# Projections and query features on half rows of the array, in a kernel of feature-map attention and a gated MLP

## The chip, the cores and the metric

The kernel runs on one core of a Trainium2 chip. The metric is the device time of one execution in microseconds. Before the change it is 278.79 us, the median of three runs (278.53 to 278.94).

## What is computed

The inputs are q, k and v for 8 batches, 8 heads, 576 tokens and 64 channels, and a projection of 64 by 128. Keys and queries are projected, the largest magnitude of a token's projection is taken off, and both signs go through the exponential, which gives 256 features.

```python
def phi(x):
    proj = np.einsum('bhsd,df->bhsf', x, w_phi)
    proj = proj - np.max(np.abs(proj), axis=-1, keepdims=True)
    return np.concatenate([np.exp(proj), np.exp(-proj)], axis=-1)
q_p, k_p = (phi(q), phi(k))
kv = np.einsum('bhsf,bhsd->bhfd', k_p, v)
z = np.sum(k_p, axis=2)
num = np.einsum('bhsf,bhfd->bhsd', q_p, kv)
den = np.einsum('bhsf,bhf->bhs', q_p, z)[..., None] + 1e-06
x = num / den                     # heads side by side: 576 x 512 a batch
h = np.maximum(x @ w_in, 0.0)     # 1024 wide: u and v
v_n = (v - mu) / np.sqrt(var + 1e-06)
v_s = np.einsum('ts,bsd->btd', w_spatial, v_n) + b_spatial[None, :, None]
out = (u * v_s) @ w_out
```

## The kernel before

The attention is cut into 36 units, listed in `units`. A *pair unit* holds two heads of one batch and 512 of its 576 tokens: for each head four blocks of 128 tokens, eight blocks in all. A *tail unit* holds the last 64 tokens of two batches for all eight heads, again eight blocks of 128 rows. There are 32 pair units and 4 tail units. The hand-written `ORDER` says what `step(i)` issues, and for which unit: each stage has a lag (`LAGS`), so that one step projects unit i, transposes the maxima of unit i - 1, makes the query features of unit i - 2 and the attention of unit i - 3. The MLP of a batch (`b_tasks`: `b_v` at L447, `b_u` at L515, `b_s` at L536, `b_o` at L561) is put into `queue` when its attention is done, and `fill(share)` issues some of it between the attention stages. The share beside each name in `ORDER` sets how much.

The stages that matter here:

- `a_transpose` (L259, L261) and `cross` bring 64 channels of two token blocks onto the 128 partitions: block 2j ("even") on partitions 0 to 63, block 2j + 1 ("odd") on 64 to 127. The result is `kT` or `qT`, four columns of blocks. For batches 0 and 1 and the tails, TensorE transposes and VectorE or ScalarE copies; from batch 2 (`XB`) a DMA on SP's queue transposes.
- `by_token` (L266) projects: one column of blocks is the stationary operand, and `wphi2`, 128 rows by 256 columns, is streamed through. Its upper left and lower right quarters hold the projection and the others zeros, so one matmul of 256 columns gives both blocks. A PSUM bank takes four blocks in token order.
- `a_keys` reads each of two key banks by a VectorE maximum (`mk`, L278) and two ScalarE exponentials (`kf`, L281). `a_scale` makes the factors of the maxima (`em`, L301) and POOL multiplies the values by them (`vs`, L306 and L308). `a_queries` takes the query maxima from two banks (`mq`, L292) and writes each as a bf16 value and its remainder into 16 columns of `mhl` (L295 and L296: VectorE in the first five units, POOL after them).
- `a_max_t` transposes `mhl` on TensorE (L327). Early and tail units copy 16 rows to `mT` (L333). The others are `merged`: the maxima are copied four times side by side into partitions of `qT` that are not needed (L330), and into those of a second arrangement of the queries, `qE` (a `qt` tile, L331), which `q_even` fills by a DMA on SP's queue one step ahead.
- `a_qfeat` projects the queries again, transposed, and takes off the maxima. A merged unit uses `wm`, which holds the projection and the rows of -1 for the maxima in one stationary operand: eight matmuls of 128 columns (L344). An early pair unit uses two matmuls of 256 columns and four of 128 per half (L348, L352), a tail unit sixteen of 128 (L357, L359). Each half fills one bank, read by two ScalarE exponentials (`qf`, L365).
- `a_kv` (L378, L380) sums keys and values, `a_num` (L398) and `tail_num` (L426) make the numerators, `norm` (L388, L389) divides, and `tail_x_t` (L439, L441) transposes the tails' result. It follows `a_qfeat` directly in the step that ends a batch.

All PSUM tiles share one tag of eight banks, which are handed out in turn. Two engines' accesses to one bank are put in an order by semaphores, two readers' as well. `pin` keeps an instruction in its place in the program, and its instructions have line L61.

The output of a batch is made by `b_o`: four matmuls of 512 columns, a copy by VectorE and ScalarE in turn (L564), and a DMA of 256 KB on SP's queue (L570). `b_o_tail` does it for the tails with two DMAs (L576). For the last batch `out_tasks` gives the four blocks and then the tails.

Of the kernel before, what the change touches and what calls it, by code (L numbers as in the profile page):

```python
# [8 lines left out]
FP32 = mybir.dt.float32  # L9
# [7 lines left out]
def kernel(  # L17
# [15 lines left out]
    nc = tc.nc  # L33
# [134 lines left out]
    wm = cpool.tile([P, H, F], BF16)  # L168
    sel1 = cpool.tile([P, H], BF16)
    sel = cpool.tile([P, H, F], BF16)  # L170
    pin(nc.vector.tensor_tensor)(out=sel1, in0=ident[:, 0:H], in1=ident[:, H:2 * H], op=ALU.add)
# [18 lines left out]

    def alternate(t, i):
        return t.rearrange("p (j two) f -> p j two f", two=2)[:, :, i, :]

    for i in range(2):
        pin(nc.scalar.copy)(out=alternate(wm, i),
                            in_=wphi2[:, i * F:(i + 1) * F].unsqueeze(1).to_broadcast([P, NP, F]))

    def maxima_rows(i):
        r = slice((1 - i) * D, (1 - i) * D + 2 * H)
        pin(nc.scalar.copy)(out=alternate(wm[r], i), in_=alternate(sel[0:2 * H], i))  # L200
# [40 lines left out]
    def merged(u):  # L241
        return u["pair"] and u["b"] >= XB

    def q_even(u):
        u["qE"] = qts[u["i"] % len(qts)]
        pin(nc.sync.dma_start)(out=u["qE"][0:D], in_=u["qT"][0:D])
# [16 lines left out]
    def by_token(xT, half):  # L263
        ps = psum.tile([P, 4, F], FP32, tag="bank", name="ps")
        for x in range(2):
            nc.tensor.matmul(out=ps[:, 2 * x:2 * x + 2, :], lhsT=xT[:, 2 * half + x, :], rhs=wphi2,  # L266
                             start=True, stop=True)
        return ps

    def a_keys(u):  # L270

        u["mk"] = small.tile([P, H], FP32, tag="mk", name="mk")
        u["kf"] = feat.tile([P, 2, H, F], BF16, tag="kf" if u["pair"] else "kf_t", name="kf",
                            bufs=4 if u["pair"] else 2)
        for half in range(2):
            pk = by_token(u["kT"], half)
            hs = slice(4 * half, 4 * half + 4)
            nc.vector.tensor_reduce(out=u["mk"][:, hs], in_=pk, axis=AX.X, op=ALU.max,  # L278
                                    apply_absolute_value=True)
            for s, sc in ((0, 1.0), (1, -1.0)):  # L280
                nc.scalar.activation(out=u["kf"][:, s, hs, :], in_=pk, func=AF.Exp, bias=0.0, scale=sc)  # L281

    def a_queries(u):

        m, early = mhl[u["i"] % NM], u["i"] < EARLY
        if not early:
            mq = small.tile([P, H], FP32, tag="mq", name="mq")
        for half in range(2):
            pq = by_token(u["qT"], half)
            if early and half == 0:  # L290
                mq = pq[:, 0, 0:H]
            nc.vector.tensor_reduce(out=mq[:, 4 * half:4 * half + 4], in_=pq, axis=AX.X, op=ALU.max,  # L292
                                    apply_absolute_value=True)
        eng = nc.vector if early else nc.gpsimd
        eng.tensor_copy(out=m[:, 0:H], in_=mq)  # L295
        eng.tensor_tensor(out=m[:, H:2 * H], in0=mq, in1=m[:, 0:H], op=ALU.subtract)  # L296
# [28 lines left out]
    def a_max_t(u):  # L325
        pt = psum.tile([P, P], BF16, tag="bank", name="pt")
        nc.tensor.transpose(out=pt, in_=mhl[u["i"] % NM], identity=ident)  # L327
        if merged(u):
            odd, even = u["qT"][0:2 * H], u["qE"][D:D + 2 * H]
            nc.vector.tensor_copy(out=odd, in_=pt[0:2 * H, :].unsqueeze(1).to_broadcast([2 * H, 4, P]))  # L330
            nc.vector.tensor_copy(out=even, in_=pt[0:2 * H, :].unsqueeze(1).to_broadcast([2 * H, 4, P]))  # L331
            return
        nc.vector.tensor_copy(out=mT[u["i"] % NM][0:2 * H, :], in_=pt[0:2 * H, :])  # L333

    def a_qfeat(u):

        m = mT[u["i"] % NM]
        u["qf"] = []
        for half in range(2):
            pq = psum.tile([P, 4, P], FP32, tag="bank", name="pq")  # L340
            if merged(u):
                for par, src in enumerate((u["qE"], u["qT"])):
                    for x in range(2):
                        nc.tensor.matmul(out=pq[:, 2 * par + x, :], lhsT=wm[:, 4 * half + 2 * x + par, :],  # L344
                                         rhs=src[:, 2 * half + x, :], start=True, stop=True)
            elif u["pair"]:
                for par in range(2):
                    nc.tensor.matmul(out=pq[:, 2 * par:2 * par + 2, :], lhsT=wphi2[:, par * F:(par + 1) * F],  # L348
                                     rhs=u["qT"][:, 2 * half:2 * half + 2, :], start=True, stop=False)
                    for x in range(2):  # L350
                        j = 4 * half + 2 * x + par
                        nc.tensor.matmul(out=pq[:, 2 * par + x, :], lhsT=sel[:, j, :], rhs=m,  # L352
                                         start=False, stop=(x == 1))
            else:
                for x in range(4):
                    h = 4 * half + x
                    nc.tensor.matmul(out=pq[:, x, :], lhsT=wphi2[:, (h % 2) * F:(h % 2 + 1) * F],  # L357
                                     rhs=u["qT"][:, h // 2, :], start=True, stop=False)
                    nc.tensor.matmul(out=pq[:, x, :], lhsT=sel[:, h, :], rhs=m, start=False, stop=True)  # L359
            if u["pair"]:  # L360
                qf = feat.tile([P, 2, 4, P], BF16, tag="qf", name="qf", bufs=7)
            else:
                qf = feat.tile([P, 2, 4, P], BF16, tag="qf_t", name="qf_t", bufs=4)
            for s, sc in ((0, 1.0), (1, -1.0)):
                nc.scalar.activation(out=qf[:, s], in_=pq, func=AF.Exp, bias=0.0, scale=sc)  # L365
            u["qf"].append(qf)
# [204 lines left out]

    def b_o_tail(g, bls):
        r = slice(bls[0] * TL, (bls[-1] + 1) * TL)
        ob = o_mm(lambda dc: gs[g]["uTt"][:, dc, r], r)
        for bl in bls:
            nc.sync.dma_start(out=out[2 * g + bl, T0:S, :], in_=ob[bl * TL:(bl + 1) * TL, :])  # L576
# [21 lines left out]
    def out_tasks(b):  # L598
        ts = [(MM, lambda j=j: b_o(b, j)) for j in range(NB)]
        if b % 2:  # L600
            ts.append((MM, lambda: b_o_tail(b // 2, [0, 1])))
        return ts

    def b_tasks(b):
# [11 lines left out]
        for y in range(NB):  # L616
# [5 lines left out]
    ORDER = (("keys", 0.375), ("queries", 0.25), ("attention", 0), ("sums", 0.25),  # L622
             ("next", 0.125), ("features", 0), ("out", 0), ("maxima", 0))
# [24 lines left out]
    def step(i):  # L648
# [5 lines left out]
        for what, share in ORDER:  # L654
            for u in units[max(0, i - 5):i + 2]:
# [3 lines left out]
                if what == "keys":  # L659
                    a_keys(u)  # L660
# [3 lines left out]
                elif what == "queries":  # L664
                    a_queries(u)
# [27 lines left out]
    at(0, maxima_rows, 0)  # L693
    at(1, load_v, 1)
    at(1, maxima_rows, 1)
# [20 lines left out]
    for u in units:  # L716
        if merged(u):
            at(u["i"] - 1, q_even, u)
# [50 lines left out]
```

## Time and profile before

| | |
|---|---|
| time, median of 3 runs | 278.79 us (278.53 to 278.94) |
| the profiled execution | 277.52 us, span 275.7 us from the first to the last instruction |
| maxima of keys and queries (L278, L292) on DVE | 72 of 681 ns; 62 of 678 and 10 of 690 ns |
| exponentials of keys and queries (L281, L365) on ACT | 144 of 638 ns; 128 of 625 and 16 of 608 ns |
| projections (L266) on PE | 288 matmuls of 128x256 |
| value scaling (L306) on POOL | 64 of 1042 ns |
| granted TensorE clock | 1.0 of full speed throughout |

PE is TensorE, DVE VectorE, ACT ScalarE, POOL GpSimd and SP SyncE. In a line of the profile the output stands left of the arrow and the inputs right of it, then the shapes, the count after an x, busy time in us and mean time in ns. A matmul's shape begins with the rows and columns of the array that its stationary operand takes (64*128 is half the rows), then partitions and columns streamed. Matmuls are pipelined: one takes some 0.2 us from start to modelled end, while the next can start long before. The timeline merges equal instructions in a row, and its second column is the time from the first one's start to the last one's end.

### The profile page before, as it was taken

What the parts mean: (1) busy time and instruction counts of PE and PEld (TensorE: products, weight loads), DVE (VectorE), ACT (ScalarE), POOL (GpSimd) and SP (SyncE); (2) the same over time, 40 slices, a digit from 0 to 9 for tenths busy, and PEclk for the clock granted to TensorE, in tenths of its full rate; (3) what the DMA queues carried; (4) which work ended last, traced back from release to release, by engine and by line L of the source; (5) the groups of instructions that cost most, each with busy time, mean ns of one, the idle gap of its engine ahead of it and who ended that gap; (6) DMA issues with size and microseconds to landing.
All of it is one profiled execution on the core that took longest, in us unless ns stands there. A gap on an engine that the chain in (4) does not pass through costs nothing.

```text
span 275.7 us, 8138 instructions
## 1 busy us (share of the span) xinstructions
PE 254.7 (92%) x3007; PEld 171.3 (62%) x3047; DVE 236.5 (86%) x614; ACT 218.1 (79%) x501; POOL 184.4 (67%) x312
## 2 busy tenths in 40 slices
PE   3778999999999999999998999999998999999993
PEld 2467776777665766666665775766655765554441
DVE  7989999879999889998889899988898897565751
ACT  7898999797698978999798979998798977633511
POOL 7999899999569945897787954997347632410200
PEclk9999999999999999999999999999999999999999
DMA  7999999999999997999999998899744301211115
GB/s 209 230 228 146 164 155 113 181 208 122 202 200 219 232 212 133 232 176 199 156 110 221 258 183 146 171 233 176 104 89 118 88 2 73 81 40 40 76 40 190
DMA packets 84840, 42.43 MB, mean 154 GB/s; under 512 B 51840, under 2 KB 80192, under 8 KB 84800
## 3 DMA queue, kind: packets, MB, share of 16 engines
q1 hardware_dynamic: 60240, 30.95, 54.5%
q0 software_dynamic: 24400, 10.89, 38.5%
q8 instruction: 24, 0.39, 0.6%
q14 instruction: 16, 0.13, 0.2%
q10 hardware_dynamic: 160, 0.07, 0.1%
HBM read 32.85 MB, written 9.44 MB: 153 GB/s over the span
## 4 chain that ended last, share of the span: by engine, by line
PE 70%; ACT 14%; DVE 11%; issue 3%; ACTq 0%; DVEq 0%
PE pv L447 10%; PE ps L536 10%; PE po L561 9%; PE pu L515 8%; PE ps L266 7%; ACT kf L281 7%; PE pv L378 4%; PE pn L398 4%; ACT qf L365 4%; DVE mk L278 3%; PE pq L344 3%; PE ps L537 2%; PE pn L426 2%; ACT vr L449 1%; PE pu L527 1%
## 5 line engine op out<-in xcount | busy, mean ns | idle before, releaser
L306 POOL TENSOR_TENSOR vs<-v_f,em 128x512 bf16<-128x512 f32 x64 | 65.4, 1042 | 27.8 <-ACT em L301 25.3
L281 ACT ACTIVATE kf<-ps 128x512 bf16<-128x512 f32 x144 | 75.4, 638 | 6.5 <-DVE mk L278 6.5
L365 ACT ACTIVATE qf<-pq 128x512 bf16<-128x512 f32 x128 | 66.6, 625 | 9.6 <-PE pq L344 7.5
L278 DVE TENSOR_REDUCE mk<-ps 128x4 f32<-128x512 f32 x72 | 46.3, 681 | 0.7
L292 DVE TENSOR_REDUCE mq<-ps 128x4 f32<-128x512 f32 x62 | 39.9, 678 | 2.2 <-PE ps L266 2.0
L561 PE MATMUL po<-w_out_bf,uT 128*128 128x512 bf16 x120 | 31.9, 379 | 1.4 <-ACT kf L281 0.8
L461 POOL TENSOR_TENSOR rs<-var,neghalf 64x1 f32<-64x1 f32 (+1 forms) x16 | 12.8, 797 | 30.5 <-DVE var L456 30.3
L536 PE MATMUL ps<-w_spT,vn 128*128 128x512 bf16 x119 | 32.5, 379 | 0.5
L450 DVE BATCH_NORM_STATS2 stats<-vr 128x6 f32<-128x512 bf16 (+1 forms) x40 | 26.7, 684 | 6.5 <-ACT vr L449 6.2
L447 PE MATMUL pv<-w_in_bf,xT 128*128 128x512 bf16 x117 | 30.7, 379 | 1.2 <-ACT kf L281 0.6
L515 PE MATMUL pu<-xT,w_in_bf 128*128 128x512 bf16 x119 | 31.1, 379 | 0.5 <-issue 0.2
L449 ACT ACTIVATE vr<-pv 128x512 bf16<-128x512 f32 (+1 forms) x40 | 23.8, 620 | 8.9 <-PE pv L447 8.1
L539 DVE TENSOR_TENSOR uT<-ps,uT 128x512 bf16<-128x512 f32 x32 | 22.0, 687 | 8.5 <-PE ps L537 7.6
L378 PE MATMUL pv<-vs,kf 128*128 128x66 bf16 x512 | 24.5, 193 | 1.3 <-ACT kf L281 1.1
L389 DVE TENSOR_TENSOR x<-pn,rc 128x256 bf16<-128x256 f32 x64 | 25.0, 416 | 0.3
L398 PEld LDWEIGHTS <-qf 128*128 128x128 bf16 x512 | 20.2, 97 | 7.4 <-issue 1.7
L517 ACT ACTIVATE uT<-pu 128x512 bf16<-128x512 f32 x32 | 19.7, 643 | 6.3 <-PE pu L515 3.2
L378 PEld LDWEIGHTS <-kf 128*128 128x128 bf16 x512 | 21.7, 97 | 3.6 <-issue 2.9
L398 PE MATMUL pn<-kv,qf 128*128 128x66 bf16 x512 | 21.9, 193 | 0.9 <-ACT kf L281 0.3
L380 PE MATMUL pv<-vst,kf 128*128 128x66 bf16 x128 | 21.2, 192 | 1.4 <-POOL vst L61 1.4
L564 ACT COPY ob<-po 128x512 f32<-128x512 f32 x18 | 11.0, 613 | 14.3 <-PE po L561 8.8
L467 POOL TENSOR_SCALAR vn<-vr,rs 128x512 bf16<-128x512 bf16 x28 | 21.2, 764 | 0.9
(130 smaller groups left out, 562.6 us busy)
## 6 DMA issues: line engine op xcount, KB each, us to landing
out_dram<-ob SPq DMA_DIRECT2D x32, 256.0 KB, 2.7
v_f<-in_v_dram SPq DMA_DIRECT2D x14, 512.0 KB, 5.6
k_bf<-in_k_dram POOLq DMA_DIRECT2D x14, 256.0 KB, 6.3
q_bf<-in_q_dram POOLq DMA_DIRECT2D x14, 256.0 KB, 5.9
qt<-qT_b SPq DMA_DIRECT2D x24, 64.0 KB, 4.2
v_tl<-in_v_dram SPq DMA_DIRECT2D x8, 128.0 KB, 5.9
v_f<-in_v_dram SPq DMA_DIRECT2D x1, 1024.0 KB, 8.8
w_in_bf<-in_moe_w_in_dram POOLq DMA_DIRECT2D x2, 512.0 KB, 7.0
```

Source lines behind the costliest of these rows:

```text
L278: nc.vector.tensor_reduce(out=u["mk"][:, hs], in_=pk, axis=AX.X, op=ALU.max, apply_absolute_value=True)
L281: nc.scalar.activation(out=u["kf"][:, s, hs, :], in_=pk, func=AF.Exp, bias=0.0, scale=sc)
L292: nc.vector.tensor_reduce(out=mq[:, 4 * half:4 * half + 4], in_=pq, axis=AX.X, op=ALU.max, apply_absolute_value=True)
L306: nc.gpsimd.tensor_tensor(out=vs[:, s, :, 0:D], in0=st[u["b"]]["v"][:, pj * H:(pj + 1) * H, :], in1=em[:, s, :].unsqueeze(2).to_broadcast( ...
L365: nc.scalar.activation(out=qf[:, s], in_=pq, func=AF.Exp, bias=0.0, scale=sc)
L378: nc.tensor.matmul(out=pv[:, hh, s, :], lhsT=u["kf"][:, s, 4 * hh + c, :], rhs=u["vs"][:, s, 4 * hh + c, :], start=(c == 0), stop=False)
L398: nc.tensor.matmul(out=pn[:, pos, :], lhsT=u["qf"][hh][:, s, pos, :], rhs=d["kv"][:, 2 * u["pj"] + hh, s, :], start=(s == 0), stop=(s == 1))
L447: nc.tensor.matmul(out=pv[r], lhsT=lhs(kc), rhs=w_in_bf[:, kc, HALF:DFF], start=(kc == 0), stop=(kc == KC - 1))
L450: nc.vector.bn_stats(out=stats[r], in_=dst[r])
L515: nc.tensor.matmul(out=pu, lhsT=w_in_bf[:, kc, dc * P:(dc + 1) * P], rhs=d["xT"][:, kc, :], start=(kc == 0), stop=(kc == KC - 1))
L536: nc.tensor.matmul(out=ps, lhsT=d["vn"][:, sp, cs], rhs=w_spT[:, sp, 0:T0], start=(sp == 0), stop=False)
L561: nc.tensor.matmul(out=po[r], lhsT=lhs(dc), rhs=w_out_bf[:, dc, :], start=(dc == 0), stop=(dc == KC - 1))
```

## The change

- **Projections on half rows.** `by_token` now takes even and odd blocks by matmuls of 64 rows and 128 columns each: rows 0 to 63 for even, 64 to 127 for odd, in turn. Even blocks go to one bank, odd ones to another. Keys and queries of a unit are projected together into four banks (`a_project`), and the stage "queries" leaves `ORDER`.
- **Readers by parity.** `a_readers` issues: maxima of the even keys on DVE, exponentials of the odd keys on ACT, maxima of the even queries, exponentials of the even keys, maxima of the odd keys, maxima of the odd queries.
- **Maxima doubled.** The maxima and remainders are written twice into `mhl` (columns 0 to 15 and 64 to 79), so that one transpose puts them on both halves of the partitions. One copy of 80 rows into `mT` follows, for every unit.
- **Query features.** All units use one form: per half, two matmuls of 64 rows and 256 columns with the projection, and four of 64 rows and 128 columns with `sel`; even and odd blocks in two banks. `wm`, `merged`, `q_even`, `qE` and the 24 transfers go.
- **Order.** The share 0.25 of "queries" moves to "maxima", behind the transpose.
- **The end.** The last batch's tails are put second among its outputs, and its last block is made in two halves of 256 columns: one copied by ACT and sent from ACT's queue, the other copied by DVE and sent from SP's.

```diff
-    def by_token(xT, half):
-        ps = psum.tile([P, 4, F], FP32, tag="bank", name="ps")
-        for x in range(2):
-            nc.tensor.matmul(out=ps[:, 2 * x:2 * x + 2, :], lhsT=xT[:, 2 * half + x, :], rhs=wphi2,
-                             start=True, stop=True)
+    def by_token(xT):
+        ps = [psum.tile([P, 4, F], FP32, tag="bank", name="ps") for _ in range(2)]
+        for j in range(4):
+            for y in range(2):
+                r = slice(y * D, (y + 1) * D)
+                nc.tensor.matmul(out=ps[y][:, j, :], lhsT=xT[r, j, :], rhs=wphi2[r, y * F:(y + 1) * F],
+                                 start=True, stop=True)
         return ps
...
+    def a_project(u):
+        u["pk"], u["pq"] = by_token(u["kT"]), by_token(u["qT"])
...
+        most(parity(mk, 0), u["pk"][0])
+        features(1)
+        most(mq[:, 0:4], u["pq"][0])
+        features(0)
+        most(parity(mk, 1), u["pk"][1])
+        most(mq[:, 4:8], u["pq"][1])
         eng = nc.vector if early else nc.gpsimd
-        eng.tensor_copy(out=m[:, 0:H], in_=mq)
-        eng.tensor_tensor(out=m[:, H:2 * H], in0=mq, in1=m[:, 0:H], op=ALU.subtract)
...
+        eng.tensor_copy(out=twice[0], in_=mq)
+        eng.tensor_tensor(out=twice[1], in0=mq, in1=twice[0], op=ALU.subtract)
...
-        if merged(u):
-            odd, even = u["qT"][0:2 * H], u["qE"][D:D + 2 * H]
-            nc.vector.tensor_copy(out=odd, in_=pt[0:2 * H, :].unsqueeze(1).to_broadcast([2 * H, 4, P]))
-            nc.vector.tensor_copy(out=even, in_=pt[0:2 * H, :].unsqueeze(1).to_broadcast([2 * H, 4, P]))
-            return
-        nc.vector.tensor_copy(out=mT[u["i"] % NM][0:2 * H, :], in_=pt[0:2 * H, :])
+        n = D + 2 * H
+        nc.vector.tensor_copy(out=mT[u["i"] % NM][0:n, :], in_=pt[0:n, :])
...
+        pqs = [psum.tile([P, 2, 2, P], FP32, tag="bank", name="pq") for _ in range(2)]
+        sides = [(par, slice(par * D, (par + 1) * D)) for par in range(2)]
         for half in range(2):
...
+            for par, r in sides:
+                nc.tensor.matmul(out=pqs[par][:, half], lhsT=wphi2[r, par * F:(par + 1) * F],
+                                 rhs=u["qT"][r, 2 * half:2 * half + 2, :], start=True, stop=False)
+            for x in range(2):
+                for par, r in sides:
+                    nc.tensor.matmul(out=pqs[par][:, half, x, :], lhsT=sel[r, 4 * half + 2 * x + par, :],
+                                     rhs=m[r], start=False, stop=(x == 1))
...
-    ORDER = (("keys", 0.375), ("queries", 0.25), ("attention", 0), ("sums", 0.25),
-             ("next", 0.125), ("features", 0), ("out", 0), ("maxima", 0))
+    ORDER = (("keys", 0.375), ("attention", 0), ("sums", 0.25),
+             ("next", 0.125), ("features", 0), ("out", 0), ("maxima", 0.25))
...
+        if b == B - 1:
+            ts = ts[:1] + ts[-1:] + ts[1:NB - 1] + [(MM, lambda: b_o_last(b, NB - 1))]
```

## The prediction

> **What bounds the kernel now.** I read the page's busy table first, then a table of busy time by stage, the timeline around single steps, the groups kept apart by shape, and the waits.
>
> ```profile
> PE 254.7 (92%) x3007; PEld 171.3 (62%) x3047; DVE 236.5 (86%) x614; ACT 218.1 (79%) x501; POOL 184.4 (67%) x312
> ```
>
> The average says "all three are full". The stages say more (columns: microseconds, then busy PE, weight loads, DVE, ACT, POOL):
>
> ```profile
> 15.00:30.00 15.00, 11.95 (x195) 9.80 (x192) 14.06 (x42) 14.29 (x39) 13.24 (x20) 1.00 0.96 169
> 90.00:120.00 30.00, 29.55 (x377) 20.38 (x380) 27.88 (x74) 26.43 (x65) 22.50 (x39) 1.00 1.18 196
> 150.00:180.00 30.00, 29.68 (x359) 20.15 (x365) 27.73 (x73) 26.97 (x65) 21.94 (x37) 1.00 1.13 198
> ```
>
> Up to 30 us ACT and DVE are full and PE waits. From 30 to 230 us PE is busy 193.3 of 200 us: it is the bound, with DVE (182.6) and ACT (173.6) close behind. So I price PE by the pace of its starts (a busy span holds the pipeline's latency) and treat DVE and ACT as slack of about 9% and 13%.
>
> ```profile
> 118.31 0.28 PE L344 MATMUL pq<-qt,wm 128*128 128x128 bf16 x2
> 118.42 0.28 PE L344 MATMUL pq<-qT_b,wm 128*128 128x128 bf16 x2
> 118.53 0.28 PE L344 MATMUL pq<-qt,wm 128*128 128x128 bf16 x2
> 118.65 0.28 PE L344 MATMUL pq<-qT_b,wm 128*128 128x128 bf16 x2
> 118.76 0.22 PE L327 MATMUL pt<-ident,mhl 128*128 128x128 bf16 x1
> 118.81 0.60 PE L266 MATMUL ps<-wphi,kT_b 128*128 128x256 bf16 x4
> ```
>
> Eight matmuls of 128 columns take 118.76 - 118.31 = 0.45 us, 0.056 each. Four of 256 columns span 0.60, one alone 0.273 (group L266), so they start (0.60 - 0.273)/3 = 0.109 apart. The weight loads hide behind them.
>
> **What the Trainium skill says.** "TensorEngine Tiling (Array Packing)", Key Properties: tiles run independently, but a change of tiling mode drains the engine. The kernel before has such changes, where the tail transposes of 64 rows stand between full-array work:
>
> ```profile
> 104.74 0.28 PE L344 MATMUL pq<-qT_b,wm 128*128 128x128 bf16 x2
> 104.95 0.29 PE L439 MATMUL pt<-ident,xt 64*128 64x64 bf16 x4
> 105.17 0.23 PE L327 MATMUL pt<-ident,mhl 128*128 128x128 bf16 x1
> ```
>
> The second L344 starts at 104.74 + 0.056 = 104.80; at its pace L439 would start at 104.85, and starts at 104.95. L439's last starts at 104.95 + 0.29 - 0.19 = 105.05, its pace is 0.03, and L327 comes at 105.17. A change costs 0.10 going in and 0.09 coming out: 0.19 us a round trip. The trace agrees and gives the price.
>
> "TensorE: Matmul & The Clock Gate", Measured speedup vs the span model: a group of row tiles lasts one matmul plus about 4 ns for each further tile; 3.07 times is measured for four. No row tiles run side by side in this trace, but column tiles do:
>
> ```profile
> 52.26 0.40 PE L236 MATMUL pt<-ident,wsp 128*128 128x128 bf16 x4
> 52.72 0.41 PE L236 MATMUL pt<-ident,wsp 128*64 128x128 bf16 x8
> ```
>
> Eight matmuls on half arrays take as long as four on the whole: they run in pairs. That is my reason to expect pairs on rows.
>
> "PSUM — Partial Sum Buffer", PSUM bank collisions raise a hardware error: two engines may not be in one bank at once, readers included, so software orders ACT behind DVE. The trace agrees:
>
> ```profile
> ACT kf L281 <- DVE mk L278: 6.5, 13, 0.8
> ```
>
> **The change part by part.** It is 36 units: 8 early pair units, 24 later ones (batches 2 to 7), 4 tail units.
>
> *Projections.* Before: 8 matmuls of 256 columns, 8 x 0.109 = 0.872 us a unit. After: 16 of 128 columns on half the rows, alternating between halves and banks. Bounds: perfect pairs 8 x 0.056 = 0.45; no pairing 16 x 0.056 = 0.90. I take the skill's 4 ns: 8 x 0.060 = 0.48 (estimate), plus one round trip 0.19 = 0.67. Gain 0.20 a unit, 36 x 0.20 = 7.3 us.
>
> *Query features.* After, for every unit, per half: a pair of 256 columns (0.109 + 0.004) and two pairs of 128 (0.120); twice that plus 0.19 is 0.656 us. Before: late units 8 x 0.056 = 0.447, so they lose 0.21 x 24 = 5.0; early pair units 4 x 0.109 + 8 x 0.056 = 0.884, gaining 0.23 x 8 = 1.8; tail units 16 x 0.056 = 0.894, gaining 0.24 x 4 = 1.0. The later units used one matmul where there are now two; the halves only pay that back.
>
> *Mode changes saved.* At a batch's end the tail transposes (L439) follow the features directly and are now in the same mode: 8 x 0.19 = 1.5 us.
>
> PE sum: -7.3 + 5.0 - 1.8 - 1.0 - 1.5 = -6.6 us. By place: before the late units start (about 60 us) 10 x 0.20 + 1.8 + two tails' 0.5 + 0.4 = 4.7; after, 26 x 0.20 - 5.0 + 0.5 + 1.1 = 1.8 us.
>
> *Maxima.*
>
> ```profile
> L331 DVE COPY qt<-pt 16x512 bf16<-16x512 bf16 x24 | 10.0, 415 | 0.4
> L330 DVE COPY qT_b<-pt 16x512 bf16<-16x512 bf16 x24 | 9.6, 399 | 4.2 <-PE pt L327 4.2
> L333 DVE COPY mT<-pt 16x128 bf16<-16x128 bf16 x12 | 2.4, 198 | 0.0
> ```
>
> 24 times 0.415 + 0.399 becomes 0.198 (80 rows instead of 16, the same elements per row): 14.8 us off DVE, none of it on the path while PE is the bound; it is slack. The doubled split is two small operations in the same number (L295, L296, 0.19 and 0.20 on POOL); twice the elements is at most the 0.209 of the 128x32 cast at L308: nothing, POOL idles 28 us for L306 alone. The transpose stays one matmul.
>
> *Transfers.* 24 copies of 64 KB (4.2 us each to land) leave SP's queue with their 0.54 us issues. SP also issues the cross transposes, value loads and outputs; they move up by that. The copies landed ahead of their use, since L344 shows no wait on DMA: 0 on the path, up to 1 us gain.
>
> *Start.* ACT loses four copies for wm: two of 0.57 at 5.74, while it would wait anyway, and two of 0.60 at 9.39 and 12.36, where ACT and DVE are the bound: -1.2. DVE gains two small additions for the selectors (0.24 each) before the first key cast, on DVE's unbroken chain: +0.5 unless the load's landing hides it. ACT's first key exponentials no longer follow DVE into the bank: -0.5. Sum -1.2.
>
> *Readers and order.* Exponentials and maxima keep number and size; strided 128-element blocks cost nothing (the alternating wm copies took 0.61, contiguous exponentials 0.63). New waits: DVE reads k0, q0, then k1, which ACT holds for two exponentials (L281, 0.638 span, 0.52 apart: 1.1 us); ACT reads k1, then k0, behind DVE's 0.68. Behind DVE's wait stand the second maxima, the split on POOL, then normalisation and statistics; PE waits for these through banks. With level engines both waits are near zero. Four banks are filled at once, and the last is read 2.7 us later; before, the query banks were drained in 1.4. Bounds: it removes ACT's 6.5 us of waits, or adds up to 1 us a unit. I take a net gain of 1 us out of the 6.7 us PE idles between 30 and 230.
>
> *The end.*
>
> ```profile
> 271.27 0.58 ACT L564 COPY ob<-po 128x512 f32<-128x512 f32 x1 [1.14 <-PE po L561]
> 271.88 1.11 SPq L576 DMA_DIRECT2D out_dram<-ob  x2
> ```
>
> The last copy becomes half as wide (0.42 by L389's 128x256) and one issue follows it, not two: -0.16 - 0.55 = -0.7.
>
> Sum on the path: start -1.2; 30 to 60 us a third of the 4.7, since DVE (27.4 of 30) and ACT (26.1) are near: -1.6; late units -1.8; waits -1.0; end -0.7: -6.3 us. Against the span of 275.7 that gives 269.4. The runs have a median of 278.79 (this execution counts 277.52 with its start and end outside the span), so 278.79 - 6.3 = 272.5.
>
> **The rivals.** (1) *No pairing.* Then projections cost 1.09 (+0.21 x 36 = 7.7), late features 0.884 + 0.19 - 0.447 = +0.63 x 24 = 15, the other units 12 x 0.18 = 2.2, less 1.5: +23 us, about 300. Against it: the banks are split by half, and the column pairs above. 8%. (2) *A new wait replaces DVE's work* (slower). DVE stands at k1's maxima while ACT is still in query exponentials or evacuations. Its slack is about 0.4 us a unit and the copies free 0.6: from an ACT lag of 1.1 us the wait reaches PE, and every further 0.1 us costs 26 x 0.1 = 2.6. At 1.4 us: +7.8 - 5.3 (the gain without the 1.0 of waits) = +2.5, 281. For it: at 118.80 to 121.19 ACT runs four query exponentials and an evacuation before the keys projected at 118.81. Against: work now stands between features and keys (the share moved to "maxima"). 12%. (3) *Little.* The bank wait eats 3 to 5 us: -2, 277. 15%. (4) *More.* PE's idle time goes and pairs are perfect (0.056): -11, 268. 10%. (5) Nothing: 3%, within 0.2%, about what a measurement here tells from no change.
>
> **The numbers.** The forecast has 52%. Faster 0.52 + 0.15 + 0.10 = 0.77; same 0.03; slower 0.12 + 0.08 = 0.20. The range of 267 to 281 leaves out the unpaired case and the far ends of (2) and (4). The forecast's own range is 269 to 275.5.
>
> **What would show it.** Right: projection and feature groups marked 64*128, starts in pairs a few ns apart, a gap near 0.1 on either side; sixteen matmuls in about 0.5 us; DVE's busy time near 222, ACT's near 216; PE still the fullest engine from 60 to 230; the chain's end shorter by 0.7. Wrong: starts 0.056 apart within a pair; DVE's k1 maxima waiting for ACT by over 1 us a unit; PE waiting for banks that ACT or DVE holds.

## The result, and the profile after

The changed kernel takes 275.74 us (median of three runs, 275.18 to 276.07), against 278.87 for the kernel before, with one run more than in the table ahead: a ratio of 0.9884, 95% interval 0.9857 to 0.9911, so 3.2 us less by the ratio. A fourth run took 280.17 us in a slower state that several kernels show at times, and such runs are left out here and below. The profiled executions have spans of 275.7 and 273.4 us, 2.3 apart; what follows is accounted against these 2.3. The forecast of 272.5 stood for 6.3.

The engines' busy times, first line of the page after:

```profile
PE 251.7 (92%) x3419; PEld 154.3 (56%) x3419; DVE 223.3 (82%) x593; ACT 215.9 (79%) x497; POOL 183.6 (67%) x312
```

DVE has lost 13.2 us, ACT 2.2, PE 3.0. The same three stages as before (microseconds, then busy PE, weight loads, DVE, ACT, POOL):

```profile
15.00:30.00 15.00, 11.72 (x189) 8.89 (x188) 12.49 (x35) 12.49 (x33) 12.63 (x18) 1.00 0.92 162
90.00:120.00 30.00, 29.00 (x410) 17.13 (x410) 25.34 (x69) 25.80 (x63) 24.34 (x41) 1.00 1.37 193
150.00:180.00 30.00, 29.98 (x428) 18.14 (x427) 25.81 (x70) 26.80 (x64) 24.42 (x40) 1.00 1.07 179
```

Later on PE is full as before, with more slack on DVE. In the first stage, though, ACT is at 12.49 of 15 where it had 14.29, and DVE at 12.49 where it had 14.06: what was full at the start is full no longer. The timeline of PE around one late unit's features and another's projections:

```profile
118.38 0.28 PE L336 MATMUL pq<-qT_b,wphi 64*128 64x256 bf16 x2
118.50 0.28 PE L340 MATMUL pq<-mT,sel 64*128 64x128 bf16 x4
...
118.93 0.23 PE L325 MATMUL pt<-ident,mhl 128*128 128x128 bf16 x1
...
119.96 0.40 PE L254 MATMUL ps<-wphi,kT_b 64*128 64x128 bf16 x8
120.19 0.39 PE L254 MATMUL ps<-wphi,qT_b 64*128 64x128 bf16 x8
120.51 0.39 PE L546 MATMUL po<-w_out_bf,uT 128*128 128x512 bf16 x1
```

Sixteen projections take 120.51 - 119.96 = 0.55 us, the change of mode behind them included; without it that is 0.46, where sixteen unpaired ones at 0.056 each would take 0.90. The single records show the two of a pair 2 to 4 ns apart and the next pair 56 ns on. Features take 118.93 - 118.38 = 0.55, again with the change of mode.

How far each unit is behind the kernel before, by the start of its key projections in the two traces:

| unit | 0 | 1 | 3 | 6 | 11 | 20 | 30 | 35 |
|---|---|---|---|---|---|---|---|---|
| start before, us | 5.76 | 8.66 | 15.19 | 30.12 | 60.75 | 118.81 | 186.22 | 219.81 |
| after minus before, us | +0.46 | +1.27 | +1.82 | +3.34 | +1.89 | +1.15 | -0.66 | -2.43 |

The change loses 3.3 us at the start, wins 1.5 between 30 and 61 us and 4.3 between there and 220. The gain is real and larger than it looks; more than half of it is paid back in advance.

### The profile page after: what moved, and what is told of

It reads as the page before. It is cut to its first block, busy times and chain, and to the rows that moved or that the text cites. A ratio compares the mean times of both kernels' runs of the same rounds, so it can differ in the third digit from the quotient of the medians.

```text
span 273.4 us, 8788 instructions
## 1 busy us (share of the span) xinstructions
PE 251.7 (92%) x3419; PEld 154.3 (56%) x3419; DVE 223.3 (82%) x593; ACT 215.9 (79%) x497; POOL 183.6 (67%) x312
## 4 chain that ended last, share of the span: by engine, by line
PE 65%; ACT 17%; DVE 8%; POOL 4%; DMA 2%; issue 2%; SPq 0%; POOLq 0%; ACTq 0%
PE ps L521 10%; PE po L546 10%; PE pv L432 9%; PE pu L500 7%; ACT qf L350 7%; ACT kf L279 6%; PE ps L254 4%; PE pv L363 4%; PE pn L383 4%; PE pq L336 3%; PE ps L522 3%; PE pq L340 2%; DVE stats L435 2%; DMA first<-in_k_dram 2%; DVE mk L275 2%
## 5 line engine op out<-in xcount | busy, mean ns | idle before, releaser
L279 ACT ACTIVATE kf<-ps 128x512 bf16<-128x512 f32 x144 | 76.3, 653 | 3.7 <-PE ps L254 3.6
L275 DVE TENSOR_REDUCE mk<-ps 128x4 f32<-128x512 f32 x72 | 49.1, 681 | 11.7 <-PE ps L254 7.0
L275 DVE TENSOR_REDUCE mq<-ps 128x4 f32<-128x512 f32 x62 | 41.1, 678 | 0.0
L521 PE MATMUL ps<-w_spT,vn 128*128 128x512 bf16 x128 | 33.1, 380 | 0.9 <-POOL vn L452 0.6
L500 PE MATMUL pu<-xT,w_in_bf 128*128 128x512 bf16 x128 | 32.2, 379 | 0.3 <-DVE mk L275 0.3
L432 PE MATMUL pv<-w_in_bf,xT 128*128 128x512 bf16 x128 | 31.8, 379 | 0.0
L434 ACT ACTIVATE vr<-pv 128x512 bf16<-128x512 f32 (+1 forms) x40 | 25.0, 629 | 7.6 <-PE pv L432 7.2
```

The source lines that it names most:

```text
L275: nc.vector.tensor_reduce(out=out, in_=ps, axis=AX.X, op=ALU.max, apply_absolute_value=True)
L279: nc.scalar.activation(out=kf[:, s].rearrange("p (j two) f -> p j two f", two=2)[:, :, y, :], in_=u["pk"][y], func=AF.Exp, bias=0.0, scale=sc)
L432: nc.tensor.matmul(out=pv[r], lhsT=lhs(kc), rhs=w_in_bf[:, kc, HALF:DFF], start=(kc == 0), stop=(kc == KC - 1))
L500: nc.tensor.matmul(out=pu, lhsT=w_in_bf[:, kc, dc * P:(dc + 1) * P], rhs=d["xT"][:, kc, :], start=(kc == 0), stop=(kc == KC - 1))
L521: nc.tensor.matmul(out=ps, lhsT=d["vn"][:, sp, cs], rhs=w_spT[:, sp, 0:T0], start=(sp == 0), stop=False)
```

## Experiments

Each is an edit of the changed kernel, except the two that say otherwise. Ratios are to the kernel before, run beside it (changed kernel: 0.9884); a difference to the changed kernel is given by the medians and, where the two disagree, by the ratios. "Unit 6" is the lag of its projections, as in the table. Two of the kernels below are the changed one until after unit 6 (late projections twice, copies put back), and their unit 6 is 3.8 and 3.9 behind: half a microsecond of this lag says nothing.

For PE, the time from each matmul's start to the next is taken apart: the pace of the first (*work*), up to 0.095 us where the tiling mode changes (62 times before, 188 after; the medians are 0.095 and 0.093), and the rest (*stalls*). Matmuls of 512 columns that some traces lack, 40 before, are counted as work at their pace.

**Is PE the bound of the late stage?** Late projections are issued twice, to the same values.

```diff
-        for j in range(4):
+        for j in [j for _ in range(times) for j in range(4)]:
...
+        n = 2 if u["i"] >= 10 else 1
+        u["pk"], u["pq"] = by_token(u["kT"], n), by_token(u["qT"], n)
```

> The changed kernel with every projection of the last 26 units issued twice into the same banks (the second result replaces the first, equal one): 16 more half-row matmuls a unit in pairs, 8 x 0.056 = 0.45 us of PE's time, with no further wait, bank or change of mode. If PE is the bound in the late units as forecast: +9 to +12 us (26 x 0.45 = 11.7). If ACT, DVE and the hand-over of banks set the pace and PE has room: +0 to +4 us.

Measured: 286.68 us, 1.0307 (1.025 to 1.0364), 10.9 us more than the changed kernel by the medians and 11.8 by the ratios, for 26 x 0.45 = 11.7 us issued. The page's first line:

```profile
PE 262.7 (92%) x3835; PEld 165.4 (58%) x3835; DVE 224.9 (79%) x593; ACT 217.6 (77%) x497; POOL 182.1 (64%) x312
```

PE's 11.0 us more are the difference of the two spans. PE's time in the late stage counts almost one for one.

**Is DVE's freed time worth something?** Two DVE copies of 16 partitions are put back in each of the 24 late units.

```diff
+        if u["pair"] and u["b"] >= XB:
+            for _ in range(2):
+                spare = small.tile([2 * H, 4, 112], BF16, tag="spare", name="spare", bufs=1)
+                nc.vector.tensor_copy(out=spare, in_=pt[0:2 * H, 0:112].unsqueeze(1).to_broadcast([2 * H, 4, 112]))
```

> The changed kernel with two copies of 16 x 448 elements from the maxima's transpose into a spare tile on DVE in each of the 24 late pair units (not used): about 0.75 us of DVE a unit, 18 us in all, in the place of the two copies that the change removed. The forecast took DVE's freed time as slack off the path: at most +1 us. Rival: DVE's time is the main part of what the late units gained: +4 us or more.

Measured: 278.34 us, 0.9998 (0.9976 to 1.0021), 2.6 us more than the changed kernel by the medians and 3.2 by the ratios; the intervals do not meet.

```profile
PE 254.6 (92%) x3419; PEld 155.8 (56%) x3419; DVE 237.2 (86%) x641; ACT 216.7 (78%) x497; POOL 183.3 (66%) x312
```

DVE's busy time is back where it was before the change (236.5). Its 13.9 us cost about 2.9, a fifth, although PE is the fullest engine: more than the forecast allowed, less than the rival.

**Does the order of the stages matter?** The maxima are transposed before the features, so that features and projections stand together in one tiling mode.

```diff
-             ("next", 0.125), ("features", 0), ("out", 0), ("maxima", 0.25))
+             ("next", 0.125), ("maxima", 0.25), ("out", 0), ("features", 0))
```

> The changed kernel with the maxima's transpose and its share of MLP work moved ahead of the query features, which then stand directly before the next unit's projections in the same half-row mode: one change of mode out and one in less a unit, 0.19 us. Theory (mode changes are on PE's path in the late units): 26 x 0.19 = -5 us, less what ACT loses by getting eight exponentials in a row, so -2 to -5. Rival (banks and ACT bound what PE can use, since the MLP work no longer stands between features and keys): 0 to +3.

Measured: 282.0 us, 1.0093 (1.0071 to 1.0116), 6 us more, beyond both expectations. In the trace the mode changes fall from 188 to 128 and cost 11.8 us instead of 17.3, as meant, but PE's stalls rise from 25.8 to 36.7. No MLP work stands between features and projections now. The wait that grows most is that of the numerators for the query exponentials that they read, from 0.2 us to 5.5 in 21 places; that banks read late add to it is not shown.

**Keys and queries in stages of their own**, with no share between them.

```diff
-    ORDER = (("keys", 0.375), ("attention", 0), ("sums", 0.25),
+    ORDER = (("keys", 0.375), ("queries", 0), ("attention", 0), ("sums", 0.25),
```

> The changed kernel with the queries' projection and maxima a stage of their own again, behind the keys' share of MLP work; the shares stay as changed (0.25 behind the maxima's transpose), and half rows, parity banks and the doubled maxima stay. It costs one more round trip of modes a unit, 0.19 us. If filling four banks at once and four maxima in a row on DVE is what the head loses by: the seventh unit's projection starts 1 to 2 us earlier than in the changed kernel, the late units lose up to 26 x 0.19 = 5 us, sum +1 to +4. If the joint stage is what the late units gain by (fewer waits between ACT and DVE): +5 us or more, with no gain in the head.

Measured: 283.03 us, 1.0162 (1.0122 to 1.0202), 7.3 us more by the medians and 7.8 by the ratios. There are 242 mode changes, which cost 22.2 us instead of 17.3, and PE's stalls grow by 3.3; the two sums come to 8.2 of the 8.5 by which the spans differ. Unit 6 is 3.9 behind, so projecting keys and queries together is not by itself what delays the start.

**Without the pairs.** All even blocks are issued before the odd ones.

```diff
-        for j in range(4):
-            for y in range(2):
+        for y in range(2):
+            for j in range(4):
```

> The changed kernel with each projection's four even blocks issued first and then its four odd ones, so that only three of the sixteen matmuls of a unit can run beside one on the other half. Theory: thirteen instead of eight slots of 0.056 us, +0.28 us a unit; on the path in the 26 late units where PE is the bound: +7 us (5 to 9). Rival (half-row matmuls do not gain from standing in pairs, or PE is not the bound in the late units): within 1 us.

Measured: 276.86 us, 0.9921 (0.99 to 0.9942). It is no test of the pairs' worth: at 121.53 sixteen projections take 0.57 us, so TensorE ran the two halves side by side all the same. The theory's 7 us did not come, and for another reason than the rival's. This is taken up at the end.

**The projections alone.** The kernel before, with the change's projections, readers and share; its features, second arrangement and transfers stay.

```diff
-                    a_keys(u)
+                    a_project(u)
+                    a_readers(u)
...
-                elif what == "queries":
-                    a_queries(u)
```

> The kernel before with the change's projections, readers and shares alone: half rows, parity banks, keys and queries together. The query features stay as before, with the merged operand, the second arrangement of the queries, its 24 transfers and its two copies of the maxima on DVE; the output's end stays as before too. By PE's account of the forecast the features' part of the change costs the late units 24 x 0.21 = 5.0 us; against it stand DVE's 14.8 us, of which the run with the copies put back gave 2.9 us for 18. So: 2 to 4 us faster than the changed kernel in the late units if PE's time decides; 1 to 4 us slower if DVE's time and the transfers do.

Measured: 275.66 us, 0.9873 (0.9839 to 0.9907), as fast as the whole change, with DVE at 236.2 us. Unit 6 is 2.4 behind, unit 35 1.1 ahead (2.4 in the changed kernel). The other half of the change, new features against fewer copies and transfers, is worth nothing that these intervals can show. The traces do tell the two kernels apart by place; this is taken up with the late units.

**The share alone.** The kernel before, with the share of "queries" moved to "maxima".

```diff
-    ORDER = (("keys", 0.375), ("queries", 0.25), ("attention", 0), ("sums", 0.25),
-             ("next", 0.125), ("features", 0), ("out", 0), ("maxima", 0))
+    ORDER = (("keys", 0.375), ("queries", 0), ("attention", 0), ("sums", 0.25),
+             ("next", 0.125), ("features", 0), ("out", 0), ("maxima", 0.25))
```

> The kernel before with one part of the change alone: the share 0.25 of MLP work moved from behind the queries to behind the maxima's transpose, so that it stands between the query features and the next keys. The forecast gave this no price. If the place of the share is a main part of the gain (it lets ACT read the query features' banks before the next keys come): -2 to -5 us against the kernel before. If not: within 1 us.

Measured: 278.91 us, 0.9984 (0.9964 to 1.0004); unit 6 is 0.3 behind. Alone, the share explains at most 1 us of the gain, and nothing of the late start.

**The start: is it the clock?** In the trace of before the first record of the full TensorE clock is at 9.96 us, in that of after at 23.07. The table ahead says 1.0 throughout because the views print 1.00 where a trace has no record. Until the first record four transposes take 0.61 us (5.26 in the chain before, 9.38 in the chain after), later 0.38 to 0.40. The Trainium skill ("TensorE: Matmul & The Clock Gate", Part 1: The HAM clock gate) has the array at half clock until it was busy for a window of some 3.4 us. The guess is that the change, which streams for a shorter time, fills that window later. Thirty-two matmuls of the identity are put ahead of everything:

```diff
+    warm = psum.tile([P, 4, P], FP32, tag="bank", name="warm")
+    for n in range(32):
+        pin(nc.tensor.matmul)(out=warm[:, n % 4, :], lhsT=ident, rhs=ident, start=True, stop=True)
```

> The changed kernel with 32 matmuls of 128 columns on the identity put on PE between 1.3 and 5 us, where it has nothing to do; their result is not used. Theory A (the head loses because PE, with half as many columns to stream, is granted its full clock at 23 us and not at 10 us): the full clock comes before 10 us, the projection of the seventh unit starts near 31.5 us instead of 33.5, and the time falls by 1.5 to 2.5 us against the changed kernel. Rival B (the head loses by the late landing of the first keys, the selector additions on DVE and the order of the reads; PE's clock is not on the path): the clock comes earlier and the time stays within 0.5 us.

Measured: 275.32 us, 0.9867 (0.9845 to 0.9889). The clock is full from 4.67 to 8.09, 3.4 us as the page has the window, and then half until 25.16; unit 6 is 2.8 behind. Inconclusive by itself.

**Or the half rows?** The first ten units project on the whole array, with banks by half.

```diff
+        if whole:
+            for j in range(4):
+                nc.tensor.matmul(out=ps[j // 2][:, 2 * (j % 2):2 * (j % 2) + 2, :], lhsT=xT[:, j, :], rhs=wphi2,
+                                 start=True, stop=True)
+            return ps
```

> The changed kernel with the projections of the first ten units on the whole array again (eight matmuls of 256 columns against the zero-padded projection, banks by half); queries stay with the keys, query features and all later units stay on half rows. Theory A (clock): PE streams as much as before in the head, the full clock comes near 10 to 12 us, and 1.5 to 2.5 us come back. Rival B: no more than the 0.2 us a unit that the halves save is lost, so the time is equal or up to 1 us longer.

Measured: 276.6 us, 0.9911 (0.9882 to 0.994). The clock is full from 13.34 (but half again from 57.71 to 61.12), unit 6 still 2.4 behind. Some 1 us of the start may hang on the two together; the time is no shorter.

**Or where the tiles lie?** Without the constants for `wm` the first loads' targets start 64 bytes off a multiple of 256, by the addresses of the built program. A pad of 448 bytes a partition puts them back.

```diff
+    pad = cpool.tile([P, 224], BF16)
```

> The changed kernel with one unused tile of 448 bytes a partition behind the selectors, so that the tiles of all later pools start where they did before the change, modulo 512 bytes (in the changed kernel they start 64 bytes further: three small selector tiles took the place of one small and one large tile). No instruction differs. Theory C (the first loads and the last stores land later because their rows no longer start on a multiple of 256 bytes in SBUF): the second load of the first keys lands near 5.6 us instead of 7.15, the unit after it starts 0.8 us earlier, the last outputs land in 2.3 to 2.7 us instead of 3.2, and the time falls by 1 to 2.5 us against the changed kernel. Rival (the landings vary for other reasons): within 0.5 us.

Measured: 276.64 us, 0.9927 (0.9899 to 0.9955). The second load of keys, for which POOL's first cast waits, lands at 5.26 us instead of 7.15 (5.58 before), and unit 6 is 3.8 behind. The load moves, the start does not, and the last output still takes 3.0 us to land (3.2 after), not the 2.3 to 2.7 expected.

**All of these at once**: the pad, a memset moved off DVE's start, the warm-up, and 16 dummy matmuls ahead of each of the first six projections.

```diff
+        for n in range(idle):
+            nc.tensor.matmul(out=ps[0][:, n % 4, :], lhsT=ident, rhs=ident, start=True, stop=True)
...
+        u["pk"], u["pq"] = by_token(u["kT"], 16 if u["i"] < 6 else 0), by_token(u["qT"])
```

> The changed kernel with three edits to its head: the pad of the run beside it; the zeroing of one value tile (0.94 us of DVE before the first key cast) put off to the eighth step; and PE kept busy, by 32 matmuls on the identity before the first unit and 16 ahead of the key projection in each of the first six units (into the bank that the projection then overwrites, while PE waits for the keys). If the head's loss is the late first casts and PE's half clock: full clock before 10 us and kept, the seventh unit starts at 30.5 us or earlier (33.5 in the changed kernel), and 2.5 to 4 us come off the changed kernel's time. If it lies in the joint projection, the new order of the reads or the banks: at most 1.5 us come off.

Measured: 276.56 us, 0.9921 (0.9898 to 0.9943). The clock is full from 6.09 to 26.57. ACT begins the keys of unit 4 only 0.7 us behind before (2.5 in the changed kernel), but those of unit 5 again 2.6 (2.6). In between, PE waits for unit 5's queries: it begins to transpose them at 24.92, when their load has landed at 24.88. One gate was opened, and the next one held.

**Is it the order of DVE's work?** In the first six units the next key transposes and their copy are issued after the second of the four maxima, not after all.

```diff
         most(mq[:, 0:4], u["pq"][0])
+        if u["i"] < 6:
+            a_transpose(unit(u["i"] + 1), "k")
         features(0)
```

> The changed kernel with one reordering in its first six units: the next unit's key transposes and VectorE's copy of them are issued after the second of the four maxima instead of after all four, so that the copy stands ahead of the maximum that waits for ScalarE's first two exponentials. Nothing else is moved. Theory, that the start is lost because each next key copy, and so the next projection and ScalarE's next exponentials, stands behind all four maxima: the projections of unit 6 start at most 1.5 us behind the kernel before instead of 3.3, ScalarE's waits for the first key projections shrink from some 1.3 us each, and the run comes out 1.5 to 2.5 us under the changed kernel, 273.4 to 274.4 us. Rival, that ScalarE's exponentials and VectorE's maxima hold each other up whatever the order of the copy (the same banks, ScalarE's share of the work, GpSimd's scales behind them): unit 6 is again 2.5 to 3.5 us behind and the time within 0.7 us of the changed kernel's.

Measured: 275.97 us, 0.9889 (0.9857 to 0.9921). Unit 2 is 0.1 ahead of before (1.6 behind in the changed kernel), unit 3 1.0 behind (1.8), unit 6 again 2.9. The rival holds. ACT's timeline shows why (in brackets its idle time and what ended it):

```profile
9.77 0.60 ACT L281 ACTIVATE kf<-ps 128x512 bf16<-128x512 f32 x1 [0.81 <-PE ps L256]
...
12.82 0.60 ACT L281 ACTIVATE kf<-ps 128x512 bf16<-128x512 f32 x1 [0.67 <-PE ps L256]
...
21.74 2.06 ACT L354 ACTIVATE qf<-pq 128x512 bf16<-128x512 f32 x4 [1.16 <-PE pq L344]
...
27.33 2.06 ACT L354 ACTIVATE qf_t<-pq 128x512 bf16<-128x512 f32 x4 [1.39 <-PE pq L344]
```

Its waits for projections shrink from 1.31 and 1.32 us to 0.81 and 0.67, and the waits for features grow: over the first seven units its gaps above 0.12 us ahead of exponentials sum to 6.4 us against 6.6 in the changed kernel and 2.3 before.

No version is shown to be faster than the changed kernel: the lowest, with the warm-up (0.9867), overlaps it widely.

## Why the prediction was right, and where not

The direction and the mechanism of the gain were right: 275.74 lies in the range, below before, and the projections in pairs, which gain as much alone, bring it. The size was not: it lies just outside the forecast's own range of 269 to 275.5, and nearer to the third rival's 277 than to 272.5. That the total came so close is in part luck, for one term had the wrong sign and another was too small. By its terms:

| term | forecast | measured |
|---|---|---|
| start (to unit 6) | -1.2 | +3.3 |
| 30 to 60 us (unit 6 to 11) | -1.6 | -1.5 |
| late units and waits (unit 11 to 35) | -1.8 - 1.0 | -4.3 |
| the end | -0.7 | +0.1 |
| sum | -6.3 | -2.3 (spans) |

**TensorE's account held.** Over all matmuls, work falls by 18.8 us and mode changes rise from 5.8 to 17.3, net -7.3; the forecast was -6.6. A unit's projections cost 0.55 with the change of mode behind them and 0.09 for the one ahead, 0.64 (forecast 0.67), its features the same (0.656). The twice-issued projections show that this time is the bound of the late stage.

**The late gain was larger, and DVE was not slack.** The forecast called DVE's 14.8 us "none of it on the path". The copies of the maxima fell from 22.0 us in three groups to the 7.6 of the group below, 14.4 less, and DVE as a whole by 13.2. PE's account between units 11 and 35 says what this time was for:

```profile
L327 DVE COPY mT<-pt 80x128 bf16<-80x128 bf16 x36 | 7.6, 210 | 2.6 <-PE pt L325 2.4
```

| units 11 to 35, us | before | changed | projections alone | copies put back |
|---|---|---|---|---|
| PE work and mode changes | 151.5 | 148.6 | 146.2 | 148.5 |
| PE stalls | 7.6 | 6.2 | 10.0 | 8.1 |
| sum | 159.1 | 154.7 | 156.2 | 156.7 |

The changed kernel's sum comes again, as 154.8, in five more traces of kernels that are the same in these units. So 2.9 of the 4.3 us are TensorE's own (forecast 1.8, since projections and features each cost 0.02 to 0.03 less a unit than priced), and 1.4 are stalls (forecast 1.0). But the stalls fall only because DVE was relieved. With the projections and their readers alone they rise to 10.0, a wait that the forecast put at nothing while it counted on 1.0 of gain. The other half of the change then gives TensorE 2.4 us more to do and takes 3.8 of stalls away, and putting copies back brings 1.9 of them again. The copies and the 24 transfers are not told apart here.

**The failing step is the start.** It priced the copies that ACT and DVE lose and gain there, and held that what leaves a full engine shortens the stage: -1.2, where +3.3 was measured. The waits between 5 and 32 us are where it went, first before, then after:

```profile
ACT kf L281 <- DVE mk L278: 1.6, 4, 0.7
```

```profile
ACT kf L279 <- PE ps L254: 3.6, 3, 1.3
...
ACT qf L350 <- PE pq L340: 1.7, 2, 1.4
```

The wait of ACT's exponentials for DVE's maxima, which the forecast hoped to remove, is gone (in the whole list too, 6.5 us before). In its place ACT waits for TensorE. DVE waits for ACT at the maxima of the odd keys: the second rival's wait, but with 4.2 us in 9 waits over the whole kernel far below the 1.1 us a unit from which it decides. ACT in the kernel before:

```profile
10.24 2.06 ACT L281 ACTIVATE kf<-ps 128x512 bf16<-128x512 f32 x4 [0.23 <-DVE mk L278]
...
13.64 2.06 ACT L281 ACTIVATE kf<-ps 128x512 bf16<-128x512 f32 x4 [0.68 <-DVE mk L278]
...
24.91 2.06 ACT L365 ACTIVATE qf_t<-pq 128x512 bf16<-128x512 f32 x4 [0.71 <-PE pq L359]
```

and after:

```profile
10.60 2.07 ACT L279 ACTIVATE kf<-ps 128x512 bf16<-128x512 f32 x4 [1.31 <-PE ps L254]
...
14.17 2.06 ACT L279 ACTIVATE kf<-ps 128x512 bf16<-128x512 f32 x4 [1.32 <-PE ps L254]
...
27.49 2.06 ACT L350 ACTIVATE qf_t<-pq 128x512 bf16<-128x512 f32 x4 [0.84 <-PE pq L340]
```

Before, ACT was kept from its next exponentials by 0.2 to 0.7 us, and at 9.39 and 12.36 it made the copies for `wm`. After, these copies are gone and ACT stands idle in their place for 1.3 us each time. The traces show three gates:

- *DVE's order.* The next key copy now stands behind all four maxima, one of which waits for ACT. The reordered kernel opens this gate for units 1 to 3.
- *A bank.* The chain of waits after (start, length, what):

```profile
24.52 1.97 ACT kf L279 x4
...
26.53 0.38 PE pt L245 x4
...
27.50 2.05 ACT qf_t L350 x4
```

ACT's last key exponential ends at 26.49, only then does TensorE transpose and make the features, and ACT is idle for 0.84 us. The chain before has such a step once, at 24.03, with 0.71 us; after it comes again at 31.57, with 0.51. The kernels with the reordering and with the projections alone have the second step too.

- *POOL's scaling.* POOL in the kernel before:

```profile
15.93 2.03 POOL L61 TENSOR_TENSOR vst<-v_tl,em 64x512 bf16<-64x512 f32 x2
```

and after, with the chain of waits behind it:

```profile
17.27 2.04 POOL L61 TENSOR_TENSOR vst<-v_tl,em 64x512 bf16<-64x512 f32 x2 [0.36 <-ACT em L299]
```

```profile
18.27 1.24 POOL vst L61 x2
...
19.56 0.21 PE pv L365
...
20.60 0.85 PE pt L245 x8
...
22.45 2.06 ACT qf L350 x4
```

The tail's scaling waits for the factors `em`, which come 1.4 us later (16.99 for 15.56). TensorE's sums of the tail wait for the scaling, the next transposes and features stand behind them, and ACT is idle for 1.41 us until 22.45. In the kernel before, the chain stays on ACT from 13.64 to 24.02.

A load hangs on the same scaling: that of unit 5's queries is issued behind it and lands at 25.29 instead of 23.98. In the changed kernel it holds nothing up, for TensorE takes the queries only at 26.53, behind the bank. It is the next gate once that one gives way: TensorE took them within 0.05 us of the landing in the kernel before and in the kernels with the head on the whole array, the projections alone and all remedies at once.

That opening one gate moves the wait to another is shown by the reordered kernel and by the one with all remedies. That opening all three would bring the 3 us back is only argued: no run opens all three. Clock, half rows, alignment, share and the joint stage are each excluded as the one cause; the first two may have a part of about 1 us. The lag is there with the projections and their readers alone (2.4), so most of it does not come from the new features. One rival is untested: the new order in which DVE and ACT read the key banks stands in every kernel here that loses the start, those with the head on the whole array, the split stages and the projections alone included, and no run gives the old order back.

**The end** became shorter in issues and not in time. The last issue after:

```profile
269.26 0.41 SPq L567 DMA_DIRECT2D out_dram<-ob  x1
```

From the last issue's end to the end of the span it is 273.4 - 269.67 = 3.7 us, before 275.7 - 272.99 = 2.7. From the start of unit 35 to the last issue's end 0.9 us were saved (forecast 0.7), and the last landings took 1.0 longer. The pad does not bring this back (3.0 us from the start of the last issue to its landing, against 3.2 after and 2.4 before), while the projections alone, which keep the old end, have 2.3: it comes with the new end and not with the shifted tiles.

## What to carry to other kernels

Half-array pairs halve the price of matmuls that waste half their rows, but each burst paid a round trip of about 0.19 us in mode changes here, so count the bursts. Standing them together saves changes and lost more in waits here. Where an in-order engine was full at the start of a kernel, work taken from it is a gain only if what feeds it is ready: follow the next unit's input back through copy, bank and load before booking the time. And the second fullest engine is not free: here a fifth of DVE's time showed in the total beside a full TensorE, and without its relief the faster projections would have given part of their gain to waits.

## What was not expected of the hardware

- **Row halves run ahead of each other.** With the four even blocks issued before the four odd ones, the trace has the odd ones starting 13 to 20 ns behind their even partners (even at 121.534, 121.600, 121.656 and 121.712), not after all four, and sixteen matmuls take 0.57 us. The program as built has the four even ones first; a record of the trace does not name its half, so that the partners are the odd ones is read from the pairs and the total. The Trainium skill ("TensorE: Matmul & The Clock Gate", Part 3, The mechanism) says that matmuls start in program order; the measurement differs and decides here.
- **The clock's grant moves with small changes.** Its first record was at 9.96 us before, 23.07 after, 13.34 with the head on the whole array, and a burst of 32 dummies brought 3.4 us of full clock and then 17.1 us of half. The kernels with the head on the whole array and without the pairs lost the full clock for 3.4 us again, from 57.7 and 57.5 us.
- **A shift of the targets by less than 256 bytes delayed a landing.** With the pad the second key load landed at 5.26 us instead of 7.15. Over all traces here it landed at 5.26 to 5.86 in the five kernels whose targets start on a multiple of 256 bytes and at 5.92 to 7.15 in the nine others, so 1.9 us is the far end and the least difference is next to nothing. The skill's "DMA: Bandwidth & Descriptors", How a descriptor splits into AXI transactions, has a read that starts off a multiple of 256 bytes begin at the boundary below and pay for bytes that it does not use. Here it is the target of a write that is shifted, which the page does not treat; the direction agrees.
